# Attention backward: DMA issues move from SP's queue to GpSimd's, and the last unit's score gradients are mostly turned by TensorE

## The chip, the cores and the metric

The kernel runs on one core of one Trainium2 chip. The metric is device microseconds of one execution, as the median of several. Durations below come from one profiled execution of the same kernel, which took 2606.8 us.

The engines are named as the profile names them: PE (TensorE, with PEld for its weight loads), DVE (VectorE), ACT (ScalarE), POOL (GpSimd) and SP (SyncE, which only issues DMAs here). Each works through its own list in order. An instruction that waits holds all that stand behind it on the same engine. SP's and POOL's DMAs go into queues of their own, and all of them end on the same 16 DMA engines.

## The reference, cut to what matters

```python
def _A_ref(x, wqkv, wo):
    B, S, D = x.shape            # 1, 2048, 576
    H = 32
    Dh = D // H                  # 18
    qkv = (x @ wqkv).reshape(B, S, 3, H, Dh).transpose(2, 0, 3, 1, 4)
    q, k, v = qkv[0], qkv[1], qkv[2]
    scores = jnp.einsum("bhqd,bhkd->bhqk", q, k) * (Dh ** -0.5)
    p = _softmax(scores, axis=-1)
    o = jnp.einsum("bhqk,bhkd->bhqd", p, v)
    return o.transpose(0, 2, 1, 3).reshape(B, S, D) @ wo
...
    g = _sigmoid((x * gate_w).sum(-1, keepdims=True))
    a = _A_ref(x, A_wqkv, A_wo)
    b = _B_ref(x, B_A_re, B_A_im, B_B_re, B_B_im, B_C_re, B_C_im, B_log_dt, B_Dskip)
    return g * a + (1 - g) * b
...
    _out, _vjp = jax.vjp(_f, A_x, A_wqkv, A_wo, B_A_re, B_A_im, B_B_re, B_B_im, B_C_re, B_C_im, B_log_dt, B_Dskip, gate_w)
    _grads = _vjp(grad_out)
```

The program returns the output of a gated sum of an attention branch and a state-space branch (`_B_ref`, a long convolution), and the gradients of twelve inputs. The change lies in the attention branch, forward and backward.

## The kernel before, in words

A first stage projects the input and writes keys, values and queries, turned, to `QKV_d` in DRAM. The attention stage follows. A last stage does the state-space branch and the projections' gradients.

**Tiles, units and steps.** The 32 heads form 8 groups of 4. A head takes 32 partitions, so a group fills 128. The 2048 queries form 4 blocks of 512. A group with one block is a *unit*: 32 units. A unit has 32 *steps*: 16 tiles of 128 keys, each in two steps of two heads. One loop over G runs through all 1024 steps (`NTOT`) and then through 39 more (`OFF`, in which the last unit's backward pass drains) and 24 that only finish. In step G the forward part works on one unit and the backward part on what stood 39 steps earlier.

**One step.** PE makes scores `P1` (`ps_P<-QaT_g,KaT_g` in the profile), ACT takes their exponentials into `PT` (L1439), PE sums `accO` with the values. For the backward part PE makes the scores again with the keys as columns (`P3`, ACT: `eb`, L1444) and the products `P2` of values and output gradients; DVE multiplies `P2` with `PT` into the score gradient `ds` (L1449), two a step. PE then works in bursts, by the step's number modulo 8 (`SLOTS`): V (`accV`), Q (`accQ`), K (`accK`), and turns. All bursts use one PSUM buffer, `accB`. Scores use a ring of two, `S`. DVE adds the sums into `dvacc`, `dqa` and `dkacc`.

**Turned score gradients.** The key burst needs `ds` turned, as `dsT`. For one key tile, `ds` holds four heads. Three of them (in three of a unit's 16 tiles, all four) are turned by a DMA transpose that SP issues (L1459); the fourth by PE in the step's burst (`turn_p`, L1109), from where DVE, or ACT in the drain, copies it (L1114). `by_pe` says how many of a pair of tiles PE turns. Part of `PT` is turned by DMA too (`PTt`, L1126).

**Loads.** Strips of 128x512 (`KaT`, `QaT`, `VaT`) come from `QKV_d` by SP, some steps ahead (`at(("pre", G), ...)` puts a function at a step's beginning). `new_unit` loads the unit's output gradient `dO`.

**A unit's end.** Two steps after a unit's last forward step, `post_forward` begins: DVE takes the reciprocal `rl` of the softmax sums (L1056) and the output `Ob`; POOL makes `dOa` (L1061) and `prod` (L1063); one step later DVE reduces `prod` to the row sums (L1069), and SP stores `Ob` to `O_d`. The turned `dOa` is what the unit's `P2` needs, a few steps on.

**Gradients out.** When `dqa` of a unit, or `dvacc` and `dkacc` of a group, are complete, `store_grad` has SP turn them (`gT`, three buffers), and a *pack* on POOL four steps later copies the 18 used columns to `dtk` (one buffer) and stores it to `dqkv_d` (L1087, L1088).

**POOL's other work.** POOL also computes the state-space branch's basis (`eops`: `et`, `eT`, `eG`, `Eo`, stored to `E_d`), which nothing in the loop waits for. `e_emit` spreads it: after each step it emits operations until the costs charged in `e_done` reach a share of the total that grows with G. Other POOL work is charged there as well (1.4 for a pack, 1.25 for the copies `put_x` and `put_gy`):

```python
want = (e_total + 270.0) * min(1.0, max(0.0, (G - 10) / (NTOT + 10)))
while e_done[1] < len(eops) and e_done[0] < want:
```

The order on each engine is the order in which this loop writes it (`manual_schedule`); the state-space stage's first loads, by SP, are written into the drain.

## Time and profile before

| | us |
|---|---|
| median of 3 runs | 2608.55 |
| lowest and highest | 2606.23, 2616.14 |
| the profiled execution | 2606.8 |
| its span, first to last instruction | 2604.8 |

A row of the profile that begins with a line number (L1061) names line, engine, operation, what is written `<-` what is read, and a count; after the bar stand the busy time of all, the mean nanoseconds of one, and the engine's idle time just before them with what ended it. In a timeline a row is start, length, engine and operation, with the idle time before it in brackets. In a list of waits a row is who waited for whom, the total, how often, and the longest. A row of the chain of waits is start, length and what. Granted clock, DMA share and GB/s end a row of busy times by stretch.

### The profile page before, as it was taken

Reading aid. Unit: us, or ns where it says so; the run is one execution under the profiler, and the core shown is the slowest. Engines: PE = TensorE matmul, PEld = TensorE weight load, DVE = VectorE, ACT = ScalarE, POOL = GpSimd, SP = SyncE. Lnnn points to the kernel's source line nnn. Section 1 sums busy time; section 2 is a strip of 40 time slices with the busy share of each in tenths; the row PEclk is TensorE's granted clock in tenths of the full one; section 3 lists DMA queues with packets and bytes.
Section 4 is the critical chain, followed back from the end, with each engine's and each line's share of the span. In section 5 each row is a group of like instructions: output and inputs, shape, how many; then the busy total and the mean of one; then the engine's idle time right before and its main releaser. Section 6 shows DMA issues by size and latency. Waiting matters only on the chain. (4 is left out here: it accounts for less than half of the span.)

```text
span 2604.8 us, 72135 instructions
## 1 busy us (share of the span) xinstructions
PE 2259.1 (87%) x28346; PEld 1160.0 (45%) x28346; DVE 2277.6 (87%) x4090; ACT 2245.1 (86%) x2744; POOL 1835.4 (70%) x2859
## 2 busy tenths in 40 slices
PE   8988888888888888888888888888886799999989
PEld 4433333333333333333333333333332699998656
DVE  4849999999899899899999989998995699999964
ACT  5589999999999899999999999999984599999211
POOL 0389988998889799889889988988841155555421
PEclk8989999999899899999999999998998799999999
DMA  7749999999999999999999999999979789997995
GB/s 234 202 123 185 180 193 199 196 184 200 198 183 190 208 185 187 197 201 175 195 209 189 182 199 199 179 196 193 174 163 218 187 248 264 266 261 239 283 252 125
DMA packets 1291627, 523.50 MB, mean 201 GB/s; under 512 B 1206433, under 2 KB 1243922, under 8 KB 1288982
## 3 DMA queue, kind: packets, MB, share of 16 engines
q1 hardware_dynamic: 1243366, 372.63, 74.8%
q0 software_dynamic: 45904, 140.73, 20.1%
q10 hardware_dynamic: 2016, 5.51, 0.7%
q8 instruction: 222, 3.64, 0.6%
q14 instruction: 119, 0.97, 0.1%
HBM read 149.42 MB, written 96.94 MB: 95 GB/s over the span
## 5 line engine op out<-in xcount | busy, mean ns | idle before, releaser
L1449 DVE TENSOR_TENSOR ds<-ps_P,PT 128x512 bf16<-128x512 f32 x2048 | 1318.9, 682 | 71.2 <-PE ps_P L30 62.7
L1439 ACT ACTIVATE PT<-ps_P 128x1024 bf16<-128x1024 f32 x1024 | 1114.1, 1089 | 16.1 <-PE ps_P L30 14.4
L1444 ACT ACTIVATE eb<-ps_P 128x896 bf16<-128x896 f32 x1024 | 998.1, 975 | 68.7 <-PE ps_P L30 67.1
L30 PE MATMUL ps_P<-dOaT,VaT_g 32*128 32x512 bf16 x2048 | 791.6, 390 | 7.5 <-DVE ds L1449 6.8
L30 PE MATMUL ps_P<-QaT_g,KaT_g 32*128 32x512 bf16 x2048 | 408.2, 388 | 200.4 <-ACT PT L1439 170.6
L507 POOL TENSOR_TENSOR et<-eG,eT 128x448 f32<-128x448 f32 x576 | 542.1, 962 | 10.8
L30 PE MATMUL ps_P<-KaT_g,QaT_g 32*128 32x384 bf16 (+1 forms) x2048 | 406.9, 365 | 4.9 <-ACT eb L1444 1.2
L30 PEld LDWEIGHTS <-KaT_g 32*128 32x128 bf16 x2048 | 162.0, 92 | 491.1 <-issue 467.4
L507 POOL TENSOR_TENSOR Eo<-et,et 128x448 bf16<-128x448 f32 x288 | 326.9, 1135 | 21.0
L30 PEld LDWEIGHTS <-QaT_g 32*128 32x128 bf16 x2048 | 107.1, 91 | 244.6 <-issue 209.6
L30 PE MATMUL accO<-PT,Vtok_g 128*32 128x512 bf16 x2048 | 214.9, 396 | 0.5 <-DVE Ob L1059 0.5
L30 PE MATMUL accV<-eb,dOa 128*32 128x384 bf16 (+1 forms) x2048 | 189.1, 375 | 8.7 <-DVE dsT L1114 7.3
L30 PE MATMUL accK<-dsT,Qtok_g 128*32 128x256 bf16 x4096 | 161.8, 279 | 35.1 <-DMA dsT<-ds 34.4
L30 PEld LDWEIGHTS <-VaT_g 32*128 32x128 bf16 x2048 | 183.7, 91 | 2.9 <-issue 2.9
L30 PE MATMUL accQ<-ds,Ktok_g 128*32 128x512 bf16 x2048 | 161.4, 392 | 25.7 <-DVE dvacc L1182 20.3
L1114 DVE COPY dsT<-turn_p 128x1024 bf16<-128x1024 bf16 (+1 forms) x216 | 138.6, 642 | 1.9 <-PE turn_p L1109 1.9
L30 PEld LDWEIGHTS <-dOa 128*32 128x32 bf16 x3072 | 79.9, 96 | 132.4 <-issue 98.1
L1109 PE MATMUL turn_p<-ident_bf,ds 128*128 128x128 bf16 x1664 | 135.0, 224 | 2.1 <-DVE gb L1200 1.0
L30 PEld LDWEIGHTS <-Qtok_g 128*32 128x32 bf16 x4096 | 88.0, 97 | 103.3 <-issue 78.0
L673 ACT COPY E1e<-etp 128x1024 bf16<-128x1024 bf16 x132 | 125.4, 1068 | 1.5 <-PE etp L672 1.5
L507 POOL TENSOR_TENSOR et<-eT 128x32 f32<-128x32 f32 (+3 forms) x288 | 115.9, 422 | 11.1
L1109 PEld LDWEIGHTS <-ds 128*128 128x128 bf16 x1664 | 98.0, 99 | 49.1 <-issue 48.9
(297 smaller groups left out, 3746.3 us busy)
## 6 DMA issues: line engine op xcount, KB each, us to landing
E_d<-Eo POOLq DMA_DIRECT2D x144, 256.0 KB, 3.6
E1n<-E_d POOLq DMA_DIRECT2D x30, 1024.0 KB, 6.9
T0w<-Kp_d SPq DMA_DIRECT2D x18, 1024.0 KB
xs<-xb_d POOLq DMA_DIRECT2D x28, 512.0 KB, 10.0
dsT<-ds SPq DMA_TRANSPOSE x512
dqkv_d<-dtk POOLq DMA_DIRECT2D x96, 72.0 KB, 4.4
Md_d<-mst SPq DMA_DIRECT2D x18, 288.0 KB
skw<-Md_d SPq DMA_DIRECT2D x72, 64.0 KB
```

The lines of the kernel that those rows point to most:

```text
L30: return nc.tensor.matmul(out, lhsT=lhsT, rhs=rhs, start=start, stop=stop, **kw)
L507: nc.gpsimd.tensor_tensor(out, a, b, op=op)
L673: copy(E_[:, 4 * q:4 * q + 4], pt_)
L1109: nc.tensor.transpose(pt_[:, x, qb, :], t_[:, qb * P:(qb + 1) * P], ident_bf)
L1114: (nc.scalar.copy if NTOT <= now[0] < NTOT + OFF else nc.vector.tensor_copy)(o_(), pt_[:, x:x + n])
L1439: nc.scalar.activation(U["PT"][i, j // 2], ps, ACT.Exp)
L1444: nc.scalar.activation(e, ps.rearrange("p x q -> p (x q)")[:, KB - KT:2 * KB], ACT.Exp)
L1449: nc.vector.tensor_tensor(U["ds"][i][:, j, :], ps, U["PT"][i, j // 2][:, j % 2, :], op=A.mult)
```

## The change

Five edits are made together:

- The key strips of all groups but the first, the query and value strips inside the loop, the output gradients `dO` and the outputs `O_d` are issued by POOL, each charged with 0.7 in `e_done`. The basis target grows from `e_total + 270` to `e_total + 370`.
- The finished key sum is written into the second half of the finished value sum's tile. One DMA turns both (`gT2`, one buffer); two packs follow, four and six steps later. The query gradient has a buffer of its own (`gT1`).
- In the last unit, the DMA turns one head of four (the first), `turn_p` the fourth as in the other tiles, and a new `turn_mid` the two in between: eight turns by PE into a buffer of the ring `S`, copied by ACT (by DVE once the drain's steps are over).
- For the last unit, `by_pe` is 2 for every pair.
- In the drain the filling matmul (`ps_P<-ident_bf,J_bf`) comes in every second step instead of in each.

What POOL does after a unit's `dOa` (here the thirteenth unit's, a group's start; `et`, `eT` and `Eo` are basis work), before:

```order
L1061 TENSOR_TENSOR dOa_1232<-dO_b,rl 128x16x18
L1063 TENSOR_TENSOR prod<-dOa_1232,Ob 128x288
L1087 COPY dtk<-gT 128x288
L1088 DMA dqkv_d<-dtk 128x4x72
L507 TENSOR_TENSOR et_15718<-eG,eT 128x448
L507 TENSOR_TENSOR Eo<-et_15718,et_15621 128x4x112
L507 TENSOR_TENSOR et_15762<-eG,eT 128x448
L507 TENSOR_TENSOR et_15803<-eG,eT 128x448
L507 TENSOR_TENSOR Eo<-et_15762,et_15803 128x4x112
L560 DMA E_d<-Eo 128x1024
```

and now:

```order
L1068 TENSOR_TENSOR dOa_1232<-dO_b,rl 128x16x18
L1070 TENSOR_TENSOR prod<-dOa_1232,Ob 128x288
L1096 COPY dtk<-gT 128x288
L1097 DMA dqkv_d<-dtk 128x4x72
L507 TENSOR_TENSOR et_15685<-eG,eT 128x448
L507 TENSOR_TENSOR Eo<-et_15590,et_15685 128x4x112
L560 DMA E_d<-Eo 128x1024
L1078 DMA O_d<-Ob 128x4x72
L507 TENSOR_TENSOR Eo<-eT,sgn 128x8x16
L1096 COPY dtk<-gT 128x288
L1097 DMA dqkv_d<-dtk 128x4x72
L1015 DMA VaT_g<-QKV_d 128x512
```

The output's store and a value strip now stand between the packs and the basis work; the next unit's `dO` follows three rows on. Between the first `dOa` and the thirty-first there are 148 such new issues (28 key, 30 query and 30 value strips, 30 of `dO`, 30 of `O_d`), of 155 in all.

SP's list at a group's start (the ninth unit's), before:

```order
L1459 DMA_TRANSPOSE dsT<-ds 128x16x128
L1083 DMA_TRANSPOSE gT<-dvacc 128x4x128
L1459 DMA_TRANSPOSE dsT<-ds 128x12x128
L1070 DMA O_d<-Ob 128x4x72
L1459 DMA_TRANSPOSE dsT<-ds 128x12x128
L1009 DMA VaT_g<-QKV_d 128x512
L1035 DMA dO_b<-dO_d 128x4x72
L1083 DMA_TRANSPOSE gT<-dkacc 128x4x128
L1459 DMA_TRANSPOSE dsT<-ds 128x12x128
L1126 DMA_TRANSPOSE PTt<-PT 128x8x128
```

and now:

```order
L1485 DMA_TRANSPOSE dsT<-ds 128x16x128
L1485 DMA_TRANSPOSE dsT<-ds 128x12x128 x2
L1091 DMA_TRANSPOSE gT<-dvacc 128x8x128
L1485 DMA_TRANSPOSE dsT<-ds 128x12x128
L1137 DMA_TRANSPOSE PTt<-PT 128x8x128
```

The plain transfers are gone from between the transposes, and one `gT` of eight blocks stands for two of four.

ACT's list in the drain, before:

```order
L1114 COPY dsT<-turn_p 128x2x512
L1444 ACTIVATE eb<-ps_P_38285 128x896
L1444 ACTIVATE eb<-ps_P_38316 128x896
L1444 ACTIVATE eb<-ps_P_38345 128x896
L629 COPY mst<-psM 128x4x128
L1114 COPY dsT<-turn_p 128x2x512
L1444 ACTIVATE eb<-ps_P_38404 128x896
```

and now, at the same place (`mst` is a copy for the next stage):

```order
L1125 COPY dsT<-turn_p 128x2x512
L1470 ACTIVATE eb<-ps_P_38269 128x896
L1470 ACTIVATE eb<-ps_P_38299 128x896
L1147 COPY dsT<-ps_turn 128x1024
L1470 ACTIVATE eb<-ps_P_38339 128x896
L629 COPY mst<-psM 128x4x128
L1125 COPY dsT<-turn_p 128x2x512
L1470 ACTIVATE eb<-ps_P_38396 128x896
L1147 COPY dsT<-ps_turn 128x1024
```

A copy of 128x1024 comes after every second exponential: 15 in all on ACT and one on DVE, for 128 turns on PE (`ps_turn`), beside 12 more in `turn_p`; 19 filling matmuls go.

The diff, cut to its core:

```diff
@@ -993,7 +993,10 @@
-                        nc.sync.dma_start(t_, strip("K", g, m * KB, KB))
+                        eng = nc.gpsimd if g else nc.sync
+                        if g:
+                            e_done[0] += 0.7
+                        eng.dma_start(t_, strip("K", g, m * KB, KB))
@@ -1006,7 +1009,10 @@
-                        nc.sync.dma_start(t_, strip(k, g, m * KB, KB))
+                        eng = nc.gpsimd if now[0] else nc.sync
+                        if now[0]:
+                            e_done[0] += 0.7
+                        eng.dma_start(t_, strip(k, g, m * KB, KB))
@@ -1032,7 +1038,8 @@
-                        nc.sync.dma_start(U["dO"].rearrange("p t a b -> p t (a b)"),
+                        e_done[0] += 0.7
+                        nc.gpsimd.dma_start(U["dO"].rearrange("p t a b -> p t (a b)"),
@@ -1067,7 +1074,8 @@
-                        nc.sync.dma_start(O_d[:, b * TPQ:(b + 1) * TPQ, 4 * g * DH:4 * (g + 1) * DH], Ob.rearrange("p t a b -> p t (a b)"))
+                        e_done[0] += 0.7
+                        nc.gpsimd.dma_start(O_d[:, b * TPQ:(b + 1) * TPQ, 4 * g * DH:4 * (g + 1) * DH], Ob.rearrange("p t a b -> p t (a b)"))
@@ -1077,16 +1085,19 @@
-                def store_grad(gb, g, which, t0):
-                    c0 = which * D + g * 4 * DH
-                    gT = work.tile([P, TPQ, 4, HP], BF, tag="gT", bufs=3, name="gT")
+                def store_grad(gb, g, whichs, t0):
+                    n = len(whichs)
+                    gT = work.tile([P, n * TPQ, 4, HP], BF, tag=f"gT{n}", bufs=1, name="gT")
                     nc.sync.dma_start_transpose(out=gT.rearrange("p t a b -> p t (a b)"), in_=gb)
-                    def pack():
+                    def pack(x):
+                        c0 = whichs[x] * D + g * 4 * DH
                         dtk = work.tile([P, TPQ, 4, DH], BF, tag="dtk", bufs=1, name="dtk")
-                        nc.gpsimd.tensor_copy(dtk, gT[:, :, :, 0:DH])
+                        nc.gpsimd.tensor_copy(dtk, gT[:, x * TPQ:(x + 1) * TPQ, :, 0:DH])
                         nc.gpsimd.dma_start(dqkv_d[:, t0:t0 + TPQ, c0:c0 + 4 * DH], dtk.rearrange("p t a b -> p t (a b)"))
-                    packs.append((now[0] + 4, pack))
+                    for x in range(n):
+                        packs.append((now[0] + 4 + 2 * x, lambda x=x: pack(x)))
+                    packs.sort(key=lambda e: e[0])
@@ -1097,9 +1108,9 @@
-                def by_pe(p):
-
-                    return {NPF: 0, NPF + 1: 1}.get(p, 2)
+                def by_pe(u, p):
+
+                    return 2 if u == units[-1] else {NPF: 0, NPF + 1: 1}.get(p, 2)
@@ -1115,15 +1126,25 @@
-                def ds_tiles(U, p):
-
-                    n = by_pe(p)
+                def ds_tiles(u, p):
+
+                    n, U = by_pe(u, p), UN[u]
...
+                def turn_mid(i):
+
+                    U = UN[units[-1]]
+                    pt_ = s_pair("turn").rearrange("p a b -> p (a b)").bitcast(BF)[:, 0:2 * KB].rearrange("p (t b) -> p t b", b=P)
+                    for x in range(2):
+                        for qb in range(TPQ):
+                            nc.tensor.transpose(pt_[:, x * TPQ + qb, :], U["ds"][i][:, 1 + x, qb * P:(qb + 1) * P], ident_bf)
+                    d_ = U["dsT", i // 2][:, i % 2, TPQ:3 * TPQ, :]
+                    return lambda: (nc.scalar.copy if now[0] < NTOT + OFF else nc.vector.tensor_copy)(d_, pt_)
@@ -1178,7 +1199,7 @@
-                            o_ = DKV[("v", g, kq)] = in_place(a_)
+                            o_ = in_place(a_)
@@ -1215,7 +1236,8 @@
-                            o_ = DKV[("k", g, kq)] = in_place(a_)
+                            DKV.pop(("k", g, kq))
+                            o_ = DKV[("v", g, kq)].bitcast(BF)[:, KB:2 * KB]
@@ -1225,7 +1247,7 @@
-                    want = (e_total + 270.0) * min(1.0, max(0.0, (G - 10) / (NTOT + 10)))
+                    want = (e_total + 370.0) * min(1.0, max(0.0, (G - 10) / (NTOT + 10)))
@@ -1385,12 +1407,12 @@
-                                    at(("pre", G + 2), lambda g=g, b=b: store_grad(UN[(g, b)].pop("dqa"), g, 0, b * TPQ))
-                                elif nm in "KV" and b == NQ - 1:
-                                    at(("pre", G + 2), lambda g=g, kq=kq, nm=nm: store_grad(DKV.pop((nm.lower(), g, kq)), g, 1 + "KV".index(nm), kq * TPQ))
+                                    at(("pre", G + 2), lambda g=g, b=b: store_grad(UN[(g, b)].pop("dqa"), g, (0,), b * TPQ))
+                                elif nm == "K" and b == NQ - 1:
+                                    at(("pre", G + 2), lambda g=g, kq=kq: store_grad(DKV.pop(("v", g, kq)).bitcast(BF), g, (2, 1), kq * TPQ))
...
-                            t_, o_ = ds_tiles(UN[(g, b)], p) if by_pe(p) else ([], [])
+                            t_, o_ = ds_tiles((g, b), p) if by_pe((g, b), p) else ([], [])
@@ -1402,7 +1424,7 @@
-                        if not r1:
+                        if not r1 and s2 % 2:
@@ -1410,6 +1432,10 @@
+                    mids = []
+                    i_ = (G - NTOT - OFF + NST - 2) // 2
+                    if 0 <= i_ < NT and (G - NTOT - OFF) % 2 == 0:
+                        mids.append(turn_mid(i_))
@@ -1450,15 +1476,15 @@
-                            nj = 3 if by_pe(i // 2) >= 2 - i % 2 else 4
-                            if U["dsn", i] == nj:
+                            nj = 1 if (g, b) == units[-1] else 3 if by_pe((g, b), i // 2) >= 2 - i % 2 else 4
+                            if j == nj - 1:
                                 p = i // 2
-                                assert j == nj - 1
+                                assert U["dsn", i] >= nj
...
-                    for e_ in tail + todo.pop(("f2", G), []):
+                    for e_ in mids + tail + todo.pop(("f2", G), []):
```

## The prediction

> **What bounds the kernel now.** I read the page first, then the busy time by stretch, then one quiet unit, then the waits of single engines.
>
> ```profile
> span 2604.8 us, 72135 instructions
> PE 2259.1 (87%) x28346; PEld 1160.0 (45%) x28346; DVE 2277.6 (87%) x4090; ACT 2245.1 (86%) x2744; POOL 1835.4 (70%) x2859
> 170.70:1875.30 1704.60, 1451.21 (x17989) 570.77 (x17989) 1576.64 (x2626) 1667.10 (x1916) 1491.88 (x2442) 0.97 1.03 191
> 1875.30:1931.10 55.80, 47.74 (x600) 18.98 (x599) 52.76 (x89) 52.98 (x62) 36.59 (x56) 1.00 0.83 174
> 1931.10:2027.30 96.20, 66.57 (x692) 24.89 (x695) 57.06 (x91) 41.41 (x48) 11.31 (x21) 0.82 0.98 207
> 2027.30:2604.80 577.50, 542.30 (x8152) 467.05 (x8152) 495.44 (x1114) 379.54 (x607) 238.29 (x228) 0.96 0.85 235
> ```
>
> The last four rows give length, then busy time of PE, PEld, DVE, ACT, POOL. I cut the span at POOL's `dOa` product, which it makes once a unit: 30 whole units (1704.60 us), one more, the drain after the last forward pass (96.20 us), and the state-space stage, which the edits don't touch. In the 30 units ACT is busy 1667.10 of 1704.60 us: ACT sets the pace. POOL, at 1491.88, seems to have 213 us free. A quiet unit shows that it has not:
>
> ```profile
> 1420.47 0.67 POOL L1061 TENSOR_TENSOR dOa<-dO_b,rl 128x288 bf16<-128x288 bf16 x1
> 1476.00 0.67 POOL L1061 TENSOR_TENSOR dOa<-dO_b,rl 128x288 bf16<-128x288 bf16 x1 [0.59 <-DVE rl L1056]
> 1420.47:1476.00 55.53, 47.52 (x606) 19.02 (x604) 52.67 (x89) 55.50 (x65) 50.35 (x89) 1.00 0.97 181
> ```
>
> The unit lasts 55.53 us and ACT is busy 55.50 of it. POOL is busy 50.35, but the only idle time in which it waited for another engine is the 0.59 us ahead of the second `dOa`. The other 4.6 us are its own turn-arounds (an issue waits for its own operand, short gaps between dependent operations). Over all 30 units:
>
> ```profile
> POOL E_d L560 <- POOL Eo L507: 41.1, 136, 1.0
> POOL dOa L1061 <- DVE rl L1056: 37.5, 22, 4.3
> POOL dtk L1087 <- DMA dqkv_d<-dtk: 28.4, 18, 3.4
> POOL dqkv_d L1088 <- POOL dtk L1087: 25.3, 83, 1.0
> POOL dtk L1087 <- DMA gT<-gb: 2.8, 1, 2.8
> POOL dtk L1087 <- DMA gT<-dvacc: 1.9, 1, 1.9
> POOL dtk L1087 <- DMA gT<-dkacc: 1.9, 1, 1.9
> ```
>
> Waits for others are 37.5 (real slack), 28.4, and 2.8 + 1.9 + 1.9 = 6.6. So POOL's own stream is 1704.6 - 37.5 - 28.4 - 6.6 = 1632.1 us, 54.4 a unit, against 55.53 for ACT. **Two engines pace this loop within about 1 us a unit.**
>
> The loop is above 30 x 55.53 = 1665.9 us by 38.7, in two kinds of stall:
>
> ```profile
> 1762.40 0.69 POOL L1063 TENSOR_TENSOR prod<-dOa,Ob 128x288 f32<-128x288 bf16 x1
> 1763.12 0.46 DVE L1069 TENSOR_REDUCE dOa<-prod 128x16 bf16<-128x288 f32 x1 [2.66 <-POOL prod L1063]
> 1766.47 0.92 ACT L1444 ACTIVATE eb<-ps_P 128x896 bf16<-128x896 f32 x1 [3.34 <-PE ps_P L30]
> 653.56 1.04 PE L30 MATMUL accK<-dsT,Qtok_g 128*32 128x256 bf16 x16 [3.29 <-DMA dsT<-ds]
> 655.18 0.92 ACT L1444 ACTIVATE eb<-ps_P 128x896 bf16<-128x896 f32 x1 [3.63 <-PE ps_P L30]
> ```
>
> In the first, POOL comes late to `prod`; DVE, which works in order, waits 2.66 us at the row sums, and ACT loses 3.34. In the second, a turned `ds` comes late because SP is crowded, and ACT loses 3.63. The change relieves the second and loads the first.
>
> **The change, part by part.** *Issues moved to POOL.* In the 30 units the order has 148 new DMA issues on POOL: 88 strips (28 key, 30 query, 30 value) and 60 of 128x4x72 (30 `dO`, 30 `O`). The nearest rows are a load of the strips' shape (`gyp`), a plain store (`o0b`) and a store of the other shape (`dqkv_d`, nanoseconds of one: least, median, most):
>
> ```profile
> L616 POOL DMA_DIRECT2D gyp<-gyb_d x14 | 8.3, 594 | 0.0
> L1828 POOL DMA_DIRECT2D out_dram<-o0b x16 | 8.7, 545 | 26.2 <-DVE o0b L1825 23.6 <-DVE dsg L1629 2.7
> L1088 POOL DMA_DIRECT2D dqkv_d<-dtk x96: 750/791/835, 252.4 to 2044.0; - x96
> ```
>
> 88 x 0.594 + 60 x 0.79 = 52.3 + 47.4 = 99.7 us. With the neighbouring prices (0.545 and 0.750; 0.79 and 0.835) it is 93 to 120. No row shows a strip on POOL; I take the row of equal shape. These issues stand in POOL's own queue, so nothing hides them: behind each wait the basis operations, the packs and the next `dOa`.
>
> The Trainium skill ("DMA: Bandwidth & Descriptors", section "SWDGE vs HWDGE vs iDMA") gives plain transfers to SP or ACT and leaves GpSimd those that accumulate, cast or are irregular. That rule speaks against this edit, and the 594 ns row agrees as far as it goes: the issue occupies POOL.
>
> *Pacing.* The target for the basis work grows by 100 units of cost while 155 x 0.7 = 108.5 are charged, so some 8.5 us of it fall behind the 30 units, into the next one, where POOL is busy 36.59 of 55.80 us. I take 9 off the loop.
>
> *Packs.* `dtk` has one buffer, and the value and key packs now come two steps apart. POOL waits 28.4 + 6.6 = 35.0 us around packs today. Closer pairs wait longer for the store; less work on SP brings `gT` sooner. I keep 35, with 15 and 50 as the ends.
>
> POOL's 30 units become 1632 - 9 + 100 + 35 = **1758 us**, 58.6 a unit, more than ACT's 55.53. From then on every unit ends when POOL reaches `dOa` and `prod`. DVE is not held until POOL is about 0.8 us late (it reduces one step later), which is won once: 1757. Against 1704.6 that is **+52 us**. The ends are 1632 - 9 + 93 + 15 = 1731 (+26) and 1632 - 9 + 120 + 50 = 1793 (+88).
>
> The key sum now lands in the second half of the value sum's tile: 32 additions by DVE as before, at no cost.
>
> *SP.* These rows, one stretch of a group's start, show what goes:
>
> ```profile
> 627.21 0.54 SPq L1070 DMA_DIRECT2D O_d<-Ob  x1
> 629.48 1.02 SPq L1009 DMA_DIRECT2D VaT_g<-QKV_d  x1
> 630.59 0.39 SPq L1035 DMA_DIRECT2D dO_b<-dO_d  x1
> 631.07 1.19 SPq L1083 DMA_TRANSPOSE gT<-dkacc  x1
> ```
>
> That is 0.54 + 1.02 + 0.39 + 1.19 = 3.1 us, the last by the merge, so the `dsT` stalls should go. They are not subtracted again: the slack they gave POOL (37.5 us at `dOa`) is spent in the 1758. What is late next is POOL.
>
> *The drain.* The last unit sends one head of four through DMA; TensorE turns the others.
>
> ```profile
> PE accK L30 <- DMA dsT<-ds: 18.6, 4, 7.0
> DVE ones_f L1479 <- DMA dsT<-ds: 10.8, 1, 10.8
> 1934.23 0.60 DVE dkacc L1219
> 1947.80 0.60 DVE dkacc L1219
> L1114 ACT COPY dsT<-turn_p 128x1024 bf16<-128x1024 bf16 (+1 forms) x8 | 7.2, 905 | 1.2 <-PE turn_p L1109 0.7
> L30 PE MATMUL ps_P<-ident_bf,J_bf 128*128 128x512 bf16 x36 | 15.1, 419 | 0.0
> 1948.45 0.62 PE turn_p L1109 x8
> 2010.63 0.64 PE accV L30 x4
> 2014.72 1.03 PE turn_p L1109 x8
> ```
>
> PE waits 18.6 us for turned `ds` here, and DVE another 10.8 before the next stage begins. Eight undisturbed steps take 1947.80 - 1934.23 = 13.57 us (chain of waits), so the 36 left take 61.1. After the last `ds` the chain runs from 2009.7 through those two bursts to 2016.5, and two key bursts with an addition follow, some 9.6 us without DMA. The floor is 70.7 of 96.2: at most 25.5 us to win. Added are 17.5 bursts of eight turns (140 / 8) at 0.62 = 10.9 us of PE, less 19 fills at 0.419 = 8.0, and 15 copies on ACT at 0.905 = 13.6 us, which is busy 41.41 of 96.20. A turn takes one of the two score buffers, so a score matmul two steps later waits for ACT's copy, and behind it on PE stand the bursts of that step. I charge 3 us of PE and 3 of ACT as lying on the path, since the rest has idle time beside it: **-20 us**. The ends are -26 and 0 (all 10.9 + 13.6 on the path).
>
> **Sum.** +52 - 20 = +32. The profiled execution took 2606.8 us (span 2604.8), 1.75 below the median of the three runs; 2608.55 + 32 = 2640.
>
> **The rivals.** *POOL has room after all (faster).* The stalls go and nothing replaces them: -38.7 in the loop, -20 in the drain, 2608.55 - 58.7 = 2550. For it: both kinds of transfer late in the rows above do go. Against it: POOL would have to stay within 1665.9 us; with 1623 of its own and no waits at packs that leaves 43 / 148 = 0.29 us an issue, and with 35 of waits 0.05, where the cheapest row has 0.545. Chance 0.13. The Trainium skill ("Perfetto Trace Analysis", section "DMA Optimizations") says that spreading DMAs over the issuing engines may help where descriptor generation is the limit; it would give this rival, and SP's crowded stretch above is such a place.
>
> *The two cancel.* Low prices and short pack waits (+26), the full drain (-25): 2610. The price decides: at about 0.55 us an issue with half of the pack waits gone. Chance 0.19.
>
> *SP now waits for POOL.* The joint `gT` has one buffer; SP must wait until POOL's second pack, six steps after the transpose, has read it, and the next comes two steps behind that. A POOL that is late by over two steps (3.4 us) holds SP and with it each `dsT` queued behind. Four such waits in each of 7 groups at 1 us come to 28: 2668. They cost only where POOL then waits too. Chance 0.10.
>
> *The forecast*, POOL paces the loop: 0.58, with its own spread of 2620 to 2660.
>
> **How the numbers follow.** A measurement of this kernel can tell 0.5% (13 us) from no change. Slower by more: 0.58 + 0.10 = 0.68; within: 0.19; faster by more: 0.13. The range leaves out the first rival and the worst prices: 2600 to 2670.
>
> **What would show it.** Right: a wait of DVE's row sums for `prod` in nearly every unit, units of 57 to 60 us, POOL hardly ever waiting for `rl` (37.5 us before), ACT idle ahead of `eb` or `PT` about 90 us in the loop, no `accK` wait for `dsT`, and a drain near 76 us. Wrong: units of 55.5 with POOL still waiting for `rl`; strips issued on POOL far below 0.5 us; or a drain that is no shorter because ACT's copies or the remaining loads hold it.

## The result, and the profile after

| | runs | median us | lowest to highest us |
|---|---|---|---|
| before | 4 | 2607.39 | 2600.46 to 2616.14 |
| after | 4 | 2675.52 | 2670.78 to 2679.13 |

The ratio after to before is 1.0258, 95% interval 1.0234 to 1.0282: the changed kernel is **2.6% slower**, some 68 us, where 32 were forecast; the time lies above the range of 2600 to 2670. The profiled execution took 2670.78 us. Of the runs further below, one of e1 (9384.92 us) and the profiled one of e4 (2640.96 us, 29 above the median of its kernel) are left out of the ratios, and e4's trace is not used.

First the page after, span and busy time of each engine:

```profile
span 2668.6 us, 72331 instructions
PE 2298.2 (86%) x28467; PEld 1164.3 (44%) x28467; DVE 2284.7 (86%) x4091; ACT 2265.4 (85%) x2760; POOL 1938.0 (73%) x3014
```

POOL's busy time grew from 1835.4 to 1938.0 us, by 102.6; that of every other engine by less than 40. Then the busy time by stretch, cut at POOL's `dOa` product as before (length, then PE, PEld, DVE, ACT, POOL, granted clock, DMA share, GB/s):

```profile
172.90:1960.30 1787.40, 1495.30 (x18005) 574.84 (x18005) 1583.13 (x2627) 1673.88 (x1917) 1580.86 (x2572) 0.94 0.97 182
1960.30:2015.60 55.30, 46.89 (x590) 18.53 (x582) 52.27 (x88) 52.48 (x61) 48.18 (x77) 1.00 0.90 173
2015.60:2094.80 79.20, 66.35 (x814) 30.50 (x817) 57.88 (x93) 55.45 (x64) 9.91 (x18) 0.96 1.00 191
2094.80:2668.60 573.80, 537.13 (x8152) 462.02 (x8147) 495.29 (x1114) 379.60 (x607) 240.06 (x231) 0.98 0.86 238
```

| stretch | before | after | difference | forecast |
|---|---|---|---|---|
| start to the first `dOa` | 170.7 | 172.9 | +2.2 | 0 |
| 30 units | 1704.6 | 1787.4 | +82.8 | +52 |
| one more unit | 55.8 | 55.3 | -0.5 | 0 |
| drain | 96.2 | 79.2 | -17.0 | -20 |
| state-space stage | 577.5 | 573.8 | -3.7 | 0 |
| span | 2604.8 | 2668.6 | +63.8 | +32 |

The loss is in the 30 units, and larger there than forecast; the drain did what was forecast within 3 us. ACT, which set the pace before, is now idle for 1787.40 - 1673.88 = 113.5 us of them (37.5 before).

What POOL waits for in the 30 units (us in total, times, longest):

```profile
POOL dtk L1096 <- DMA dqkv_d<-dtk: 55.3, 27, 5.5
POOL dOa L1068 <- DVE rl L1063: 8.1, 7, 2.2
```

The waits at packs for the last pack's store grew from 28.4 to 55.3 us, those at `dOa` for `rl` shrank from 37.5 to 8.1. Both totals at `dOa`, here and in the prediction, also count the wait ahead of the first `dOa`, which ends where the 30 units begin: 4.1 us before, 2.2 after. Within the 30 units they are 33.4 and 5.9; the totals of the runs below hold such a wait too, of 2 to 5 us. What is left, 1787.4 - 55.3 - 5.9 = 1726.2 us, is POOL's own stream (the strips' two waits, 0.8 us, in it). Before, it was 1704.6 - 33.4 - 28.4 - 6.6 = 1636.2, where the prediction read 1632; by its working after would then have 1636 - 9 + 100 = 1727.

That the loop now follows POOL shows at DVE's row sums, which wait for `prod` in the 30 units, before and then after:

```profile
DVE dOa L1069 <- POOL prod L1063: 8.8, 7, 2.7
```

```profile
DVE dOa L1076 <- POOL prod L1070: 62.5, 19, 7.2
```

One stall from end to end, in the timeline of after (start, duration, engine, line, what; in brackets the idle time ahead and its releaser). It lies in the 13th unit, in which the value and key sums of the group before are packed, and which took 66.9 us here, and 57.8, 58.5 and 63.0 us in three executions of the kernel before:

```profile
910.36 0.42 POOL L1096 COPY dtk<-gT 128x288 bf16<-128x288 bf16 x1 [1.64 <-DMA dqkv_d<-dtk]
911.08 0.78 POOL L1097 DMA_DIRECT2D dqkv_d<-dtk  x1 [0.29 <-POOL dtk L1096]
...
915.26 0.63 POOL L1015 DMA_DIRECT2D QaT_g<-QKV_d  x1
915.88 1.24 POOL L1318 DMA_DIRECT2D gyb_d<-gyr_d  x1
917.12 0.44 POOL L1096 COPY dtk<-gT 128x288 bf16<-128x288 bf16 x1
917.86 0.77 POOL L1097 DMA_DIRECT2D dqkv_d<-dtk  x1 [0.29 <-POOL dtk L1096]
924.16 0.43 POOL L1096 COPY dtk<-gT 128x288 bf16<-128x288 bf16 x1 [5.53 <-DMA dqkv_d<-dtk]
...
949.09 0.46 DVE L1076 TENSOR_REDUCE dOa<-prod 128x16 bf16<-128x288 f32 x1 [6.96 <-POOL prod L1070]
952.44 0.92 ACT L1470 ACTIVATE eb<-ps_P 128x896 bf16<-128x896 f32 x1 [7.64 <-PE ps_P L30]
```

Read it downwards: the pack at 917.12 starts its store at 917.86; the next pack, two steps on, may not overwrite the one `dtk` buffer until that store has landed. No other operation stands between the two in POOL's list here, so POOL is ready for it at 918.63; the store lands some 6.3 us after its start, and POOL stands 5.53 us. It has no slack to make this good, so 25 us later `prod` is late, DVE's row sums wait 6.96 us for it, and ACT 7.64 us behind them.

### The profile page after: what moved, and what is told of

Same layout as the page of the kernel before. It is cut to its first block, busy times and chain, and to the rows that moved or that the text cites. A ratio compares the mean times of both kernels' runs of the same rounds, so it can differ in the third digit from the quotient of the medians.

```text
span 2668.6 us, 72331 instructions
## 1 busy us (share of the span) xinstructions
PE 2298.2 (86%) x28467; PEld 1164.3 (44%) x28467; DVE 2284.7 (86%) x4091; ACT 2265.4 (85%) x2760; POOL 1938.0 (73%) x3014
## 5 line engine op out<-in xcount | busy, mean ns | idle before, releaser
L1475 DVE TENSOR_TENSOR ds<-ps_P,PT 128x512 bf16<-128x512 f32 x2048 | 1325.1, 685 | 83.6 <-PE ps_P L30 71.5
L30 PE MATMUL ps_P<-dOaT,VaT_g 32*128 32x512 bf16 x2048 | 807.1, 399 | 53.3 <-DVE ds L1475 52.1
L30 PE MATMUL ps_P<-QaT_g,KaT_g 32*128 32x512 bf16 x2048 | 419.1, 397 | 197.3 <-ACT PT L1465 169.4
L30 PE MATMUL ps_P<-KaT_g,QaT_g 32*128 32x384 bf16 (+1 forms) x2048 | 415.6, 373 | 5.0 <-ACT eb L1470 0.8
L30 PE MATMUL accO<-PT,Vtok_g 128*32 128x512 bf16 x2048 | 220.4, 406 | 1.9 <-DMA Vtok_g<-QKV_d 1.4
L30 PE MATMUL accV<-eb,dOa 128*32 128x384 bf16 (+1 forms) x2048 | 196.8, 389 | 5.0 <-DVE dsT L1125 3.9
L1096 POOL COPY dtk<-gT 128x288 bf16<-128x288 bf16 x96 | 41.0, 427 | 115.2 <-DMA dqkv_d<-dtk 75.3
```

The costliest lines, as they stand in the source:

```text
L30: return nc.tensor.matmul(out, lhsT=lhsT, rhs=rhs, start=start, stop=stop, **kw)
L1475: nc.vector.tensor_tensor(U["ds"][i][:, j, :], ps, U["PT"][i, j // 2][:, j % 2, :], op=A.mult)
```

## The experiments

Three theories stood against each other. **Theory 1**: POOL's stream plus its waits at packs is the length of the loop. **Theory 2**: SP, waiting for POOL's packs at the one joint buffer, brings the turned `ds` late, and that is the loss. **Theory 3**: the issues as such cost all of it. All ratios are to runs of the kernel before on the same chip, whose medians were 2602.83 (e1 to e4), 2604.13 (e5 to e8) and 2606.26 (e9 to e12). A ratio differs from the quotient of the two medians by up to 0.25%; where us are given for a ratio, they are rough to that extent.

**The change taken apart: e1 to e4.** Each part alone on the kernel before, and the whole without the moved issues.

e1, the last unit's turns alone: the edits of `by_pe`, `ds_tiles`, `turn_mid`, `nj` and the filler, nothing else.

```
-                def by_pe(p):
+                def by_pe(u, p):
...
-                    return {NPF: 0, NPF + 1: 1}.get(p, 2)
+                    return 2 if u == units[-1] else {NPF: 0, NPF + 1: 1}.get(p, 2)
...
-                            nj = 3 if by_pe(i // 2) >= 2 - i % 2 else 4
+                            nj = 1 if (g, b) == units[-1] else 3 if by_pe((g, b), i // 2) >= 2 - i % 2 else 4
```

> The kernel before with the last unit's turns alone (no issue moved, no joint transfer). All theories: the drain loses what it lost in the whole change, 17 us, and the 30 units stay at 1704.6 within 5 us: about 2590 us (2585 to 2598), ratio 0.993. If the drain gain needed the other two parts (SP free of issues, one transfer instead of two), the drain stays above 88 us and the time above 2600.

2598.5 us, ratio 0.9978 (0.9961 to 0.9994). The windows of its profile, the 30 units and the drain:

```profile
171.50:1887.30 1715.80, 1455.72 (x17989) 570.56 (x17989) 1576.81 (x2626) 1667.77 (x1916) 1492.79 (x2442) 0.97 1.02 189
1943.10:2026.70 83.60, 67.91 (x814) 30.63 (x817) 57.99 (x92) 55.62 (x64) 10.42 (x19) 0.94 0.98 183
```

The drain lost 96.2 - 83.6 = 12.6 us by itself, so it needs neither other part; though it gave less than the 17 us expected. The loop was 11 us longer in this execution, against the 5 us allowed, and the time fell by only 6 us by the ratio (4 between the medians). e13 to e16 below take that up.

e2, the moved issues alone (strips, `dO`, `O`, their charges and the target of +370; drain and transfers as before):

```
-                        nc.sync.dma_start(t_, strip(k, g, m * KB, KB))
+                        eng = nc.gpsimd if now[0] else nc.sync
+                        if now[0]:
+                            e_done[0] += 0.7
+                        eng.dma_start(t_, strip(k, g, m * KB, KB))
...
-                        nc.sync.dma_start(O_d[:, b * TPQ:(b + 1) * TPQ, 4 * g * DH:4 * (g + 1) * DH], Ob.rearrange("p t a b -> p t (a b)"))
+                        e_done[0] += 0.7
+                        nc.gpsimd.dma_start(O_d[:, b * TPQ:(b + 1) * TPQ, 4 * g * DH:4 * (g + 1) * DH], Ob.rearrange("p t a b -> p t (a b)"))
...
-                    want = (e_total + 270.0) * min(1.0, max(0.0, (G - 10) / (NTOT + 10)))
+                    want = (e_total + 370.0) * min(1.0, max(0.0, (G - 10) / (NTOT + 10)))
```

> The kernel before with the strips, O and dO on POOL's queue alone. Theory 1 (POOL's own queue paces the loop: 100 us of issues in 1632 us of its stream): 1723 of its own plus about 30 to 35 us of waits at packs in the 30 units, so 1753 to 1760, +50 us: 2655 to 2662. Theory 2 (the joint transfer with one buffer makes SP wait for POOL's packs, and the late turned ds are the loss): most of the 83 us is absent without it, the loop at most +30: below 2640. Theory 3 (the issues as such cost the whole 83): 2685 to 2695 with the old drain.

2661.07 us, ratio 1.0209 (1.0186 to 1.0233), so +54 us (58 between the medians). Its 30 units, and POOL's waits in them:

```profile
170.70:1932.10 1761.40, 1487.59 (x18007) 572.51 (x18005) 1581.58 (x2627) 1671.60 (x1917) 1577.42 (x2571) 0.95 1.00 184
```

```profile
POOL dtk L1095 <- DMA dqkv_d<-dtk: 32.6, 20, 2.9
POOL dOa L1068 <- DVE rl L1063: 9.1, 6, 3.8
```

1761.4 us: theory 1 within 2 us, with the pack waits near where they were. Without the joint transfer most of the loss is there all the same, which theory 2 excludes; and it is not all of the 83, as theory 3 has it.

e3, the joint transfer and its packs alone:

```
-                    packs.append((now[0] + 4, pack))
+                    for x in range(n):
+                        packs.append((now[0] + 4 + 2 * x, lambda x=x: pack(x)))
...
-                            o_ = DKV[("k", g, kq)] = in_place(a_)
+                            DKV.pop(("k", g, kq))
+                            o_ = DKV[("v", g, kq)].bitcast(BF)[:, KB:2 * KB]
```

> The kernel before with value and key sums in one transfer, packs two steps apart, alone. Theory 1: POOL still has its 37.5 us of slack at the output gradients, so 20 us of longer pack waits are absorbed: 30 units within 10 us of 1704.6, 2605 to 2618. Theory 2: SP waits for the packs all the same, and turned ds come late at each group's first unit: +20 to +30, 2628 to 2640.

2622.09 us, ratio 1.0065 (1.0044 to 1.0085), +17 us (19 between the medians). The time lies between what the two theories said, and the loop's +23 us where theory 2 had it.

```profile
171.80:1899.30 1727.50, 1462.82 (x17989) 569.53 (x17989) 1577.72 (x2626) 1668.51 (x1916) 1492.93 (x2442) 0.96 1.01 188
```

```profile
POOL dtk L1088 <- DMA dqkv_d<-dtk: 54.4, 26, 5.0
POOL dOa L1061 <- DVE rl L1056: 38.6, 20, 5.4
```

The pack waits go from 28.4 to 54.4 us with no issue moved, so packing in pairs makes them. Theory 2's mechanism does not show in it: PE waited 13.3 us for turned `ds`, against 15.9 before, while DVE's waits for `prod` grew from 8.8 to 24.7 us. But theory 1 was wrong about the slack. POOL still waits 38.6 us at `dOa`: its slack did not absorb the new waits, because they fall for the most part in other units than the slack. Adding up the unit lengths shows where (us; the 7 are the 5th, 9th, and so on to the 29th, in which most packs of the value and key sums fall):

| kernel | mean of these 7 units | mean of the other 23 |
|---|---|---|
| before | 59.8 | 55.9 |
| e3, joint transfer alone | 62.2 | 56.2 |
| e2, issues alone | 61.5 | 57.9 |
| after | 65.1 | 57.9 |

On average the issues cost 2 us a unit, the pairs of packs 2 to 4 us in one unit of four.

e4, after without the moved issues (turns and joint transfer, target +270):

```
-                        nc.gpsimd.dma_start(O_d[:, b * TPQ:(b + 1) * TPQ, 4 * g * DH:4 * (g + 1) * DH], Ob.rearrange("p t a b -> p t (a b)"))
+                        nc.sync.dma_start(O_d[:, b * TPQ:(b + 1) * TPQ, 4 * g * DH:4 * (g + 1) * DH], Ob.rearrange("p t a b -> p t (a b)"))
...
-                    want = (e_total + 370.0) * min(1.0, max(0.0, (G - 10) / (NTOT + 10)))
+                    want = (e_total + 270.0) * min(1.0, max(0.0, (G - 10) / (NTOT + 10)))
```

> The changed kernel with every issue back on SP and the planner's old target (+270): last unit's turns and joint transfer stay. Theory 1: the loop falls from 1787 to about 1705 to 1715 and the drain stays at 79 to 82: 2588 to 2600. Theory 2: the loop keeps 20 to 30 us of its loss: 2610 to 2625.

2611.99 us, ratio 1.0029 (1.0011 to 1.0047). That is the sum of e1 and e3 (-0.22% and +0.65% give +0.43%) within the intervals, and not the gain that theory 1 had promised: the cost of the pairs stays. The time lies in theory 2's band (2610 to 2625); it was e5 and e6 that then decided between the two. The three parts add up: -0.22 + 2.09 + 0.65 = 2.52%, where the whole has 2.58.

**What in POOL's time it is: e5 and e6.** e5 gives the packs of the changed kernel a second buffer; the room comes from the query sum, whose last addition now writes over itself:

```
-                        o_ = U["dqa"] = grad_tile()
+                        o_ = U["dqa"] = in_place(a_)
...
-                        dtk = work.tile([P, TPQ, 4, DH], BF, tag="dtk", bufs=1, name="dtk")
+                        dtk = work.tile([P, TPQ, 4, DH], BF, tag="dtk", bufs=2, name="dtk")
```

> The changed kernel with two pack buffers (the query sum's last addition writes in place, which frees the room). Theory 1 (POOL's stream plus its waits at packs is the length of the loop): the waits at packs for the store fall from 55 us to under 15, the loop from 1787 to 1735 to 1750, and the time from 2673 to 2620 to 2635. Theory 2 (SP's waits for the packs are what costs): SP waits as before or more, the time within 10 us of 2673. If the issues as such hold the loop (theory 3), the same.

2626.35 us, ratio 1.0087 (1.0058 to 1.0117): some 45 us of the 68 are gone. Its 30 units, and the waits of POOL, SP's queue and PE in them:

```profile
171.80:1911.20 1739.40, 1473.89 (x18015) 571.77 (x18015) 1581.01 (x2629) 1671.47 (x1918) 1577.01 (x2571) 0.96 1.01 187
```

```profile
POOL dOa L1068 <- DVE rl L1063: 15.9, 7, 6.6
POOL dtk L1096 <- DMA gT<-dqa: 3.2, 1, 3.2
SPq L1091 <- POOL dtk L1096: 23.9, 15, 3.4
PE accK L30 <- DMA dsT<-ds: 15.8, 14, 3.6
```

The wait for the store is gone and the loop is 48 us shorter, as theory 1 says. In the changed kernel the last two rows read:

```profile
SPq L1091 <- POOL dtk L1096: 40.7, 18, 5.6
PE accK L30 <- DMA dsT<-ds: 19.0, 11, 3.5
```

SP's waits for packs fell by 17 us, but the key products' wait for turned `ds`, through which theory 2 would act, by 3 only: it accounts for some 3 of the 48 us. The query sum's edit comes with the second buffer and was not run alone; e10 below makes the same two edits where no issue was moved, and they brought nothing there.

e6 takes basis work out of the 30 units instead, by a slower pace of the planner:

```
-                    want = (e_total + 370.0) * min(1.0, max(0.0, (G - 10) / (NTOT + 10)))
+                    want = (e_total + 370.0) * min(1.0, max(0.0, (G - 10) / (NTOT + 45)))
```

> The changed kernel with the planner's pace for the basis work stretched over 35 more steps: some 55 us of POOL's basis work leaves the 30 units for the last unit and the drain, where POOL is busy 48 of 55 and 10 of 79 us. Theory 1: the loop falls by 45 to 55 us, drain and last unit grow by under 8: 2622 to 2638. Theory 2 and 3: issues, packs and SP stay as they are, so at most 15 us are won: 2658 or more.

2629.05 us, ratio 1.0108 (1.0075 to 1.0142). Its 30 units and its drain, then POOL's waits in the 30 units:

```profile
171.60:1909.40 1737.80, 1461.58 (x18009) 571.08 (x18008) 1578.97 (x2627) 1668.49 (x1917) 1526.74 (x2495) 0.96 1.00 186
1967.10:2050.00 82.90, 69.26 (x781) 30.88 (x781) 55.92 (x89) 54.47 (x62) 57.10 (x92) 0.86 0.92 196
```

```profile
POOL dtk L1096 <- DMA dqkv_d<-dtk: 59.6, 29, 4.9
POOL dOa L1068 <- DVE rl L1063: 18.1, 12, 3.3
```

POOL is busy 54 us less in the 30 units (1580.86 to 1526.74), and the loop is 49.6 us shorter, with the issues, the packs and SP's list as they were. In the drain POOL goes from 9.9 to 57.1 us of work; the drain grows by 3.7 us and the unit before it by 2.4. This is the most direct evidence that POOL paces the loop: 54 us of work taken from it alone shorten it by nearly as much.

**Each kind of issue alone: e7 and e8** (kernel before; only the strips, or only `dO` and `O`, on POOL's queue).

```
-                    want = (e_total + 270.0) * min(1.0, max(0.0, (G - 10) / (NTOT + 10)))
+                    want = (e_total + 330.0) * min(1.0, max(0.0, (G - 10) / (NTOT + 10)))
...
-                        nc.sync.dma_start(t_, strip("K", g, m * KB, KB))
+                        eng = nc.gpsimd if g else nc.sync
...
+                        eng.dma_start(t_, strip("K", g, m * KB, KB))
```

(e7, with the same for the query and value strips; e8 moves `dO` and `O` as e2 does, with +310.)

> The kernel before with the strips alone on POOL's queue (88 issues of 0.575 us, 51 us, in the 30 units), all else as before. Theory 1 with POOL's old slack of 37.5 us spent first: the loop +10 to +20, 2612 to 2624. If every issue costs its full price from the first on: +29 (half of the 54 that both kinds cost), 2630 or more.

> The kernel before with the output gradients' loads and the outputs' stores alone on POOL's queue (60 issues of 0.787 us, 47 us, in the 30 units). Theory 1 with the old slack spent first: +8 to +18, 2610 to 2622. If every issue costs its full price: +26, 2628 or more.

2636.37 us, ratio 1.0127 (1.0096 to 1.0158), and 2623.6 us, ratio 1.0082 (1.0052 to 1.0111). The first is a miss for "slack spent first" and lies where every issue costs its full price; the second lies between the two, 1.6 us above "slack spent first". Together they cost 2.09%, what both cost in e2. The 30 units of e7, then of e8, and POOL's wait at `dOa` in each:

```profile
169.50:1903.20 1733.70, 1472.28 (x17991) 570.71 (x17989) 1579.30 (x2626) 1669.29 (x1916) 1535.12 (x2516) 0.96 1.03 187
```

```profile
170.30:1890.90 1720.60, 1460.20 (x17989) 570.00 (x17989) 1577.80 (x2626) 1668.31 (x1916) 1534.08 (x2490) 0.97 1.03 189
```

```profile
POOL dOa L1067 <- DVE rl L1062: 16.9, 9, 4.1
```

```profile
POOL dOa L1062 <- DVE rl L1057: 13.8, 9, 3.6
```

Half of the issues use up some 20 and 22 of the 33 us of slack in the 30 units and still lengthen the loop by 29 and 16 us. Slack summed over 30 units is not one account: a unit with 4 us to spare lends nothing to a unit with none.

**Better than both: e9 to e12.** If POOL's length is all that matters, the drain's gain can be had without the loss. e9 is e1 with the slower pace of e6 on the old target of +270; e10 is e1 with e5's two buffers; e11 has both; e12 is the changed kernel with both.

```
-                    want = (e_total + 270.0) * min(1.0, max(0.0, (G - 10) / (NTOT + 10)))
+                    want = (e_total + 270.0) * min(1.0, max(0.0, (G - 10) / (NTOT + 45)))
```

> Last unit's turns alone, every issue on SP, separate transfers, and the planner's pace stretched by 35 steps (some 50 us of basis work leave the 30 units). Theory 1: POOL's own stream falls from 1630 to 1580 us and POOL is late only in a group's first unit; the loop goes from 1710 to 1685 to 1695, the time from 2598 to 2575 to 2590. If what is left in the loop comes from late turned ds and from packs, which the pace doesn't touch: 2593 or more.

> Last unit's turns alone, every issue on SP, separate transfers, and two pack buffers (query sum in place). Theory 1: the 29 us of waits at packs for the store go, some 10 to 15 us of which stood on the path in the groups' first units: 2580 to 2592. If they were all covered: within 5 us of 2598.

> Turns, two pack buffers and stretched pace together, every issue on SP. Theory 1: POOL is never late; the loop is 30 units of ACT's 55.5 (1666) and some 15 us of late turned ds: 1680 to 1688, the time 2565 to 2582.

> The changed kernel with two pack buffers and the stretched pace: issues stay on POOL, transfers joint. Theory 1 (only the length of POOL's stream counts): 1713 - 55 + 20 = 1678 of POOL against ACT's 1666 and some late ds: loop 1685 to 1700, 2575 to 2592, within 10 us of the same kernel with its issues on SP. If issues on POOL also cost by where they stand (ahead of the products that DVE waits for): 2600 or more.

| run | median us | ratio to before (95%) | 30 units us | drain us |
|---|---|---|---|---|
| e9, turns + slower pace | 2585.21 | 0.9908 (0.9888 to 0.9929) | 1699.5 | 83.8 |
| e10, turns + two buffers | 2597.66 | 0.9961 (0.9936 to 0.9986) | 1711.4 | 84.0 |
| e11, turns + both | 2587.35 | 0.9918 (0.9898 to 0.9939) | 1691.0 | 86.2 |
| e12, changed kernel + both | 2593.19 | 0.9925 (0.9900 to 0.9950) | 1708.9 | 80.7 |

The 30 units of e9 and, in the second fence, POOL's waits there:

```profile
170.30:1869.80 1699.50, 1444.42 (x17989) 569.03 (x17989) 1576.71 (x2626) 1666.34 (x1916) 1445.16 (x2361) 0.98 1.03 190
```

```profile
POOL dOa L1061 <- DVE rl L1056: 66.7, 25, 6.0
POOL dtk L1087 <- DMA dqkv_d<-dtk: 39.8, 19, 5.0
```

e9's time is in its band, its loop 4.5 us above. With 48 us less of POOL's work than in e1 the pack waits grow to 39.8 us and hold up little, since POOL has 66.7 us of slack: DVE waits for `prod` 4.2 us in all, and the 23 units without packs now average 55.5 us, ACT's own pace. What remains, 1699.5 against 30 x 55.53 = 1666, is in the 7 units with packs (60.3 us on average). e10 shows the other side: two buffers without a lighter POOL bring nothing that can be told from e1. That is a miss for the 10 to 15 us that were to stand on the path, and fits waits at packs that were covered there and were not in e5. e11 ended 5 us above its band and is not distinguished from e9.

e12 is the test of the whole: the changed kernel, with every issue still on POOL, is no longer slower than before once POOL has room for them, but 0.75% **faster**.

```profile
171.00:1879.90 1708.90, 1457.73 (x18023) 572.39 (x18027) 1579.23 (x2629) 1670.55 (x1919) 1526.21 (x2495) 0.97 1.03 189
```

Two edits turn +2.58% into -0.75%, some 80 to 87 us, which theory 3 excludes. What is gained on the kernel before is the drain: the loop is as long as there (1708.5 us in the mean of three executions, below). It is above what was expected (1685 to 1700), the time 1 us above its band. Against e11, which has its issues on SP, the intervals overlap, so nothing shows that SP's relief is worth anything. e11's loop is 18 us shorter in the one execution profiled, more than executions of one kernel differ by below (up to 11 us), so a cost that the issues keep in the loop is not excluded.

**Does the drain's gain cost something in the loop? e13 to e16.** The kernel before and e1's kernel, unchanged, two more executions of each.

> The kernel before, a second look. If the loop differs between executions: 30 units anywhere from 1695 to 1718 us, drain 96 within 1, and the wait of the key products for turned ds differs with it. If executions agree: 1704.6 within 2.

> Last unit's turns alone, a second look. If the loop differs between executions: 30 units anywhere from 1695 to 1718 us, overlapping those of the kernel before; drain 84 within 1.5. If the turns lengthen the loop: 1716 within 2 again.

> The kernel before, a third look: 30 units from 1695 to 1718 us if executions differ, 1704.6 within 2 if they agree; drain 96 within 1.

> Last unit's turns alone, a third look: 30 units from 1695 to 1718 us if executions differ, 1716 within 2 if the turns lengthen the loop; drain 84 within 1.5.

| execution | 30 units us | drain us | span us | PE's key products waiting for `dsT`, whole span, us |
|---|---|---|---|---|
| before, first | 1704.6 | 96.2 | 2604.8 | 34.4 |
| before, e13 | 1709.9 | 97.3 | 2609.5 | 38.3 |
| before, e15 | 1710.9 | 95.6 | 2608.7 | 39.6 |
| turns alone, e1 | 1715.8 | 83.6 | 2601.0 | 32.2 |
| turns alone, e14 | 1704.5 | 81.2 | 2591.1 | 22.9 |
| turns alone, e16 | 1704.8 | 82.3 | 2591.0 | 20.1 |

The loop's mean is 1708.5 us before and 1708.4 with the turns; single executions of one kernel differ by up to 11 us, and in the turns' three the longest loop goes with the longest wait for turned `ds`. Nothing shows that the turns lengthen the loop. Three of these four drains lie outside their narrow bands (97.3; 81.2 and 82.2), so the drain differs by some 2 us as well. The drain's gain is 96.4 - 82.4 = 14.0 us by these means, the spans differ by 13.3. The timed runs of e1 gave 6 us (2 to 10); why the profiled executions show more was not settled.

## Why the prediction was wrong

The sign, the bound and the mechanism were right; the size of the loop's loss was not, and the term that failed is POOL's waits at packs: 35 us taken, 15 to 50 allowed, 55.3 measured. The loop's 1787.4 us still lie within the ends that the working gave (1731 to 1793); the stated range left the worst end out, and the time lies above it.

*Two engines pace the loop.* Right: POOL became the bound, and e6 shows that in the changed kernel its length is what counts. Of the signs named ahead, DVE's waits for `prod` came in 19 of the 30 units rather than in nearly every one, and POOL hardly waited for `rl`. 23 units averaged 57.9 us, as said, and the 7 with most packs 65.1; ACT was idle for 113.5 us rather than 90.

*Prices of the issues.* Right, as the groups of after show (busy us, mean ns of one):

```profile
L1042 POOL DMA_DIRECT2D dO_b<-dO_d x32 | 25.2, 788 | 2.8 <-DMA dO_d<-eb 2.4 <-issue 0.3
L1078 POOL DMA_DIRECT2D O_d<-Ob x32 | 25.1, 786 | 2.7 <-issue 2.7
L1015 POOL DMA_DIRECT2D VaT_g<-QKV_d x32 | 18.2, 569 | 0.6 <-PE ps_P L30 0.6
L1015 POOL DMA_DIRECT2D QaT_g<-QKV_d x31 | 18.1, 584 | 0.7 <-issue 0.4 <-PE ps_P L30 0.2
L999 POOL DMA_DIRECT2D KaT_g<-QKV_d x28 | 16.2, 578 | 0.0
```

569 to 584 ns where 594 were taken from the row of equal shape, 786 and 788 where 790 were. POOL's own stream came out at 1726 against 1727 by the working, or 1723 as it stands there. Where the issues stood alone, the loop was 1761.4 us against the 1757 that the working had for them. The Trainium skill ("DMA: Bandwidth & Descriptors", section "SWDGE vs HWDGE vs iDMA") keeps plain transfers off GpSimd, and e2's +2.09% agrees, in a kernel whose GpSimd has no time to spare; where it has some, e12 (0.9925) shows that the same issues fit.

*Packs: the step that failed.* "Closer pairs wait longer for the store; less work on SP brings `gT` sooner. I keep 35, with 15 and 50 as the ends." The two effects were set against each other and taken to cancel, and neither was worked out. They don't: the waits for `gT` were 6.6 us in all and went to nothing, while the waits for the store went from 28.4 to 55.3, above the upper end. The landing times of the store (KB of one, median us), before and after, could have told most of it:

```profile
dqkv_d<-dtk POOLq DMA_DIRECT2D x96, 72.0 KB, 4.4
```

```profile
dqkv_d<-dtk POOLq DMA_DIRECT2D x96, 72.0 KB, 4.6
```

A copy starts its store 0.72 us later (911.08 - 910.36 in the timeline above), so the buffer is free 0.72 + 4.4 = 5.1 us after the copy's start; two steps are 3.4 us. As an estimate that is 1.7 us of wait for each of 28 pairs in the 30 units, 48 us, or 1.9 and 54 with the 4.6 of after, where 55.3 were measured. That the total fits so well is in part luck. By the order of the packs in POOL's timeline, 38.6 us fell at the second pack of a pair, in 19 of the 28 and with 0.7 to 5.5 us each; the other 16.7 us fell at the query sum's pack and at the pack behind it, which stand three steps apart. What POOL has to do between two packs, and how long the store takes, decides each wait.

The waits are +20 us of the 31 that were missing in the loop, and e3 (28.4 to 54.4) and e5 (to nothing, loop -48) show it from both sides.

*Slack.* The sum took POOL's waits at `dOa` as spent in full, and read them 4.1 us too high, so that POOL's stream began that much too low. Of the 33.4 us, 5.9 were left, in six units; what held those was not settled. That is 10 us more, and with the 20 of the packs it makes up the 31. e7 and e8 show with half of the load that slack is not spent in full. Against the mean of three executions of the kernel before (1708.5 us) the loop grew by 79 us rather than 83, and executions of one kernel differ by up to 11 us, so of these terms only the packs' 20 us stand clear.

*"The `dsT` stalls should go."* Wrong as a statement: PE's wait for turned `ds` in the 30 units was 15.9 us before and 19.0 after. With the issues alone it was 7.8, with the joint transfer alone 13.3, in e9, with SP's load as before, 18.7. The row of e2:

```profile
PE accK L30 <- DMA dsT<-ds: 7.8, 10, 2.1
```

Three executions of the kernel before had 15.9 to 18.7, so SP's relief in e2 was real, and the changed kernel lost it again; its SP stood 40.7 us behind POOL's packs (6.3 before). This is the rival "SP now waits for POOL" at work. Late packs are a part of its cause only: in e5, without waits for the store, SP still stands 23.9 us and PE waits 15.8; the rest of the cause stays open. It cost little beyond the terms above, which add up to the loop without it.

*The drain.* Forecast -20, measured -17.0 in the whole change and -14.0 alone: near, but in part by luck. The working let all the waiting for DMA go (25.5 us at most) and charged 6 us for the added turns and copies. Two waits for turned `ds` are left, PE's and DVE's:

```profile
PE accK L30 <- DMA dsT<-ds: 6.2, 2, 4.0
```

```profile
DVE ones_f L1505 <- DMA dsT<-ds: 6.6, 1, 6.6
```

They were 18.6 and 10.8. DVE's are not to be added to PE's, as the prediction does in words: its 10.8 us, up to 2027.31, cover PE's last two waits of 5.2 and 5.3, which end at 2020.89 and 2027.23. PE had one more wait before, for the turned `PT`:

```profile
PE accV L30 <- DMA PTt<-PT: 3.5, 1, 3.5
```

It is gone after, so 18.6 + 3.5 - 6.2 = 15.9 us of PE's waiting went, nearly the whole 17.0. The added turns and copies show no cost on the path, where 6 us were charged, and 6.2 us of waiting stayed, where none was expected: two errors that cancel.

*The rest.* +2.2 at the start and -3.7 in the state-space stage lie within what executions of one kernel differ by (168.8 to 175.8 us at the start, 573.7 to 579.4 us in that stage, e1's kernel in three executions).

## What to carry to other kernels

An engine that seems to have time (POOL was busy for 70% of the span, and for 1491.88 of 1704.60 us of the loop) may have little to spare: take its waits for others, sorted by the unit in which they fall, and spend slack only in the unit that has it. Moving a DMA's issue to an engine that computes puts the issue into that engine's stream, so first make the room (here a planner's pace, one number), then move. And when two users of one buffer are moved closer together, compare the time from copy to landing with what the engine has to do between the two before calling it even.

## What the runs showed that was not expected

The drain's turns cost PE little: PE made 814 instead of 692 matmuls there in 66.35 us of busy time instead of 66.57, at a granted clock of 0.96 instead of 0.82. In the other drains profiled (e4's aside) it was 63.7 to 66.9 us at 0.81 to 0.88 without the turns, and 66.4 to 69.7 us at 0.86 to 0.97 with them. In the 30 units the clock by and large went with the stalls too: 0.94 after, 0.95 in e2, 0.97 before, 0.98 in e9, and PE's busy time for nearly the same instructions with it, 1495.30, 1487.59, 1451.21 and 1444.42 us. In these figures the stretches in which PE waits less have the higher clock; which of the two causes the other, no run here separates.
